# Slot attention and GELU FFN on one core: gelu's first casts move from VectorE to ScalarE, other copies change engine, and the pinned first order is rearranged

## Chip, cores and metric

The kernel runs on one core of a Trainium2 chip. The metric is the device time of one execution in microseconds (us).

## What is computed

There are 8 batches of 8 heads, 576 positions, a head width of 64 and 32 memory slots per head. A softmax over the positions of `phi` gives weights `a`, which sum up `k` and `v` into 32 slots per head. Every position of `q` then attends over these slots. The attention's output, 4608 rows of 512, goes through a feed-forward layer with the exact gelu:

```python
a = exp(phi - max(phi, axis=2)); a = a / (sum(a, axis=2) + 1e-9)
k_m = einsum('bhsm,bhsd->bhmd', a, k); v_m = einsum('bhsm,bhsd->bhmd', a, v)
s = q @ k_m.T / sqrt(64); attn = softmax(s, axis=-1)
x = rows of (attn @ v_m)             # (8*576, 8*64)
h = x @ w_in                         # (4608, 2048)
out = (0.5 * h * (1 + erf(h / sqrt(2)))) @ w_out      # (4608, 512)
```

All inputs are float32 but the two weight matrices, which the kernel receives as float64 numbers viewed as 64-bit integers.

## The kernel before

**Main loop.** For each batch b, `w_in` is first multiplied by the 32 slots of `v` of each head, which gives U (2 x 128 rows, 2048 columns). The product of the attention's probabilities p with U is then h. This is cut along the 2048 columns into 16 steps f of 128 columns. A step (b, f) does the following, with its names in the order:

- `h.b.f.0` and `h.b.f.1` (L679): two halves of 288 positions, each 6 matmuls of 128x288 into one of two PSUM buffers. Six, because a float32 product is made of three products of rounded parts: p_hi U_hi, p_lo U_hi, p_hi U_lo, over two halves of the heads.
- `gelu.b.f.0`, `gelu.b.f.1` (L689, L691, L692): ScalarE writes gelu of the halves to `gf`. The last 64 positions of each batch go to `tails`, and are projected later for two batches together.
- `gh.b.f` (`gelu_hi`, which calls `copy`, L154): a cast of the 128x512 `gf` to the rounded type fp32r.
- `gl.b.f` (L698): VectorE subtracts, gl = gf - gh. There are two buffers each of `gf`, `gh` and `gl`.
- `p.b.f` (`project`, L711): 12 matmuls of 128x512, for each of four blocks of 128 positions gh wo_hi, gh wo_lo and gl wo_hi in this order. They add into the PSUM banks acc0 to acc3.

**Order of the steps.** The steps come as (b=0, f 0 to 7), (b=1, f 0 to 7), (b=0, f 8 to 15), (b=1, f 8 to 15), and then batches 2 to 7 with all 16. After f=7 of batches 0 and 1 the four banks are evicted as partial sums (`o.b.j.7`, tile `part`, L154), and added to the later result when that is evicted.

**What is made once, in the first 140 us.** For each f the loaded weights (`Lwi.f`, `Lwo.f`, into `raw`) are decoded in two 512-wide halves. `dB.f.k` are two ScalarE activations on a half (L201, L202), `dC.f.k` two VectorE steps (L206, L207), `dS.f.k` a shift (L213) on VectorE, `dDi.f` and `dDo.f` an addition on GpSimd each (L223). `dE.f` casts wo_hi (`copy`, ScalarE), and `dF.f` subtracts to get wo_lo (VectorE, L229). There are two buffers `y` for this (tag "wy"). The slots of batches 0 and 1 are made as well: transposes of a (`at`) and their copies (`atc`), `slots`, `km`, `slotsT`, `kT` (for batch 0 into `k_blocks`), and the softmax of the scores (`n_...` for batch 0 in three parts; `score`, `sT`, `max` to `mul`, `pT`, `ph`, `pl` for batch 1). Pieces of U are `Up.b.f.n` (matmuls into the PSUM tile `pu`, n columns of 128; L440), `Uh` (cast, `copy`, ScalarE) and `Ul` (subtraction, VectorE, L642). `pu`, the scores and `slotsT` share one PSUM buffer, "at".

**Who sets the order.** The string START lists the pieces of this part one by one. A piece issues its instructions when it is reached, and for the instructions of this list each engine is chained to go in just this order. Behind the list, a plan with due times and the loop over the steps place the rest, and they are the same in both kernels. A piece may carry an engine's letter behind a colon (d for VectorE, a for ScalarE, p for GpSimd). It replaces the usual engine wherever the piece goes through `eng` or `copy`:

```python
    def eng(usual):
        return {"d": nc.vector, "a": nc.scalar, "p": nc.gpsimd}[st["engine"] or usual]
...
    def gelu_hi(b, f):
        copy("d", g_of("gh", b, f), g_of("gf", b, f))
...
    def do(x):
        x, _, st["engine"] = x.partition(":")
```

A GpSimd `dD` reads what VectorE's `dC` and `dS` wrote. A `dE` waits for that addition, and a `dF` for `dE`; the `y` buffer is free for another f after the `dF`.

Of the kernel before, what the change touches and what calls it, by code (L numbers as in the profile page):

```python
# [19 lines left out]


START = """
Lphi.0.0 Lphi.0.1 Lkv0.1.0 amax.0.0 aexp.0.0 at.0.0.0 Lkv0.0.0 amax.0.1 at.0.0.4 Lq.0.0
Lwi.0 aexp.0.1 at.0.1.4 atc.0.0.4 at.0.1.0 atc.0.1.4 anorm.0 atc.0.0.0 Lwo.0 Lq.0.1
atc.0.1.0 Lwi.1 slots.0.1.0 slots.0.0.0 km.0.0.0 km.0.1.0 slotsT.0.0 kT.0.0 dB.0.0
dC.0.0 n_score.0 Lwo.1 dB.0.1 dC.0.1 n_max.0 n_sub.0 Lkv0.0.1 Lkv0.1.1 dS.0.1 dDo.0
n_exp.0 dB.1.0 n_score.1 n_score.2 dS.0.0 n_sum.0 Lphi.1.1 Lphi.1.0 n_inv.0 n_mul.0
n_T.0 n_max.1 dDi.0 dE.0 slots.0.0.1 slots.0.1.1 n_sub.1 dB.1.1 Lwi.2 dC.1.0 dC.1.1
Lwo.2 dS.1.1 dS.1.0 n_max.2 n_exp.1 n_sum.1 Lkv.1.0.4 n_sub.2 dDo.1 dDi.1 dE.1 Lwo.3
n_exp.2 km.0.0.1 km.0.1.1 slotsT.0.1 kT.0.1 amax.1.1 aexp.1.1 dF.0 Up.0.0.1 Uh.0.0  # L30
amax.1.0 n_inv.1 Ul.0.0 n_mul.1 Lkv.1.1.2 dB.2.0 Up.0.1.1 dC.2.0 Lwi.3 aexp.1.0 Uh.0.1
Lkv.1.0.2 Ul.0.1 n_T.1 dF.1 n_hi.0 dS.2.0 n_sum.2 n_lo.0 Lkv.1.0.0 at.1.0.0 n_inv.2
at.1.1.0 dB.2.1 Lkv.1.0.1 h.0.0.0 dB.3.1 Lkv.1.0.3 dC.2.1 n_hi.1 atc.1.0.0 atc.1.1.0
dDi.2 n_mul.2 n_T.2 at.1.0.4 dS.2.1 Lkv.1.1.3 dB.3.0 n_hi.2 atc.1.0.4 n_lo.1 dDo.2
at.1.1.4 atc.1.1.4 anorm.1 Lwi.4 gelu.0.0.0 n_lo.2 h.0.0.1 dC.3.1 gelu.0.0.1 slots.1.0
gh.0.0 Lkv.1.1.1 dC.3.0 h.0.1.0 km.1.0 dE.2 Up.0.2.1 dS.3.1 Uh.0.2 gl.0.0 Lkv.1.1.0
Lkv.1.1.4 Ul.0.2 dS.3.0 dDo.3 dE.3 dF.2 p.0.0 slots.1.1 dB.4.0 dC.4.0 gelu.0.1.0 Lwo.4
h.0.1.1 Lq.1.0 km.1.1 dDi.3 Lwi.5 dB.4.1 dF.3 slotsT.1 kT.1 h.0.2.0 dC.4.1 dS.4.1 dDo.4
Up.0.3.1 Lwo.5 gelu.0.1.1 gelu.0.2.0 Uh.0.3 dS.4.0 gh.0.1 Ul.0.3 h.0.2.1 gl.0.1 dE.4
Lwi.6 dB.5.0 dDi.4 h.0.3.1 gelu.0.2.1 gh.0.2 score.1.0 Lq.1.1 sT.1.0.1 p.0.1 h.0.3.0  # L40
sT.1.0.0 gelu.0.3.1 Lwo.6 Lwi.7 dC.5.0 dB.5.1 dF.4 Up.0.4.1 dS.5.0 gelu.0.3.0 gl.0.2
max.1.0 gh.0.3 Uh.0.4 p.0.2 sub.1.0 exp.1.0 dDi.5 Ul.0.4 dC.5.1 Up.0.5.1 dS.5.1 dDo.5
h.0.4.1 h.0.4.0 Uh.0.5 dB.6.0 gl.0.3 gelu.0.4.0 Ul.0.5 p.0.3 sum.1.0 dC.6.0 inv.1.0
dS.6.0 gelu.0.4.1 mul.1.0 dDi.6 Lwo.7 score.1.1 h.0.5.1 pT.1.0 gh.0.4 dE.5 sT.1.1.1
ph.1.0 h.0.5.0 Lwi.8 dB.6.1 gelu.0.5.0 sT.1.1.0 gl.0.4 gelu.0.5.1 Up.0.6.1 dC.6.1 gh.0.5
Uh.0.6 dS.6.1 Lwi.9 dF.5 p.0.4 Ul.0.6 dDo.6 dB.7.1 max.1.1 Lwo.9 Up.1.0.4 h.0.6.0 dB.7.0
gl.0.5 Uh.1.0 sub.1.1 dC.7.0 dS.7.0 Ul.1.0 h.0.6.1 pl.1.0 dC.7.1 dE.6 gelu.0.6.0 dDi.7
gelu.0.6.1 dS.7.1 exp.1.1 Lwo.8 p.0.5 gh.0.6 dDo.7 Up.0.7.1 Uh.0.7 gl.0.6 Ul.0.7 sum.1.1
h.1.0.0 inv.1.1 dF.6 h.0.7.0 gelu.0.7.0 dE.7 Up.1.4.4 mul.1.1 dB.8.0 pT.1.1 h.0.7.1
gelu.1.0.0 dC.8.0 ph.1.1 gelu.0.7.1 pl.1.1 p.0.6 h.1.0.1 h.1.1.1 dF.7 gh.0.7 dB.8.1  # L50
gl.0.7 dC.8.1 gelu.1.0.1 dB.9.1 h.1.1.0 gh.1.0 p.0.7 dB.9.0 dS.8.1 gelu.1.1.0 o.0.1.7
dC.9.1 dS.9.1 h.1.2.0 gelu.1.1.1 dS.8.0 Lwi.12 dDo.8 h.1.2.1 Lwi.11 o.0.0.7 dDo.9
o.0.3.7 gl.1.0 Lwo.11 o.0.2.7 dE.9 dC.9.0 p.1.0 dE.8 gelu.1.2.1 gh.1.1 dDi.8 gelu.1.2.0
dF.8 h.1.3.0 dS.9.0 gl.1.1 gh.1.2 dB.11.1 dDi.9 gelu.1.3.0 Lwi.10 h.1.3.1 Lwo.10 dF.9
p.1.1 dC.11.1 Uh.1.4 dS.11.1 gl.1.2 gelu.1.3.1 dB.11.0 gh.1.3 dB.10.0 Ul.1.4 dDo.11
p.1.2 h.1.4.1 h.1.4.0 Lwo.12 gelu.1.4.1 dC.11.0 Lwi.13 gelu.1.4.0 dS.11.0 dC.10.0
# [3 lines left out]
gelu.1.6.1 h.1.7.1 dS.12.0 gh.1.6 dDo.12 gl.1.5 gelu.1.7.1 h.1.7.0 p.1.5 Ul.0.8 gl.1.6  # L60
Lwi.15 dE.12 dB.13.1 h.0.8.0 dDi.12 dF.12 dC.13.1 gelu.1.7.0 h.0.8.1 dB.14.1 dC.14.1
dB.14.0 gh.1.7 gelu.0.8.0 gelu.0.8.1 p.1.6 dS.13.1 Lwo.15 Up.1.8.4 dDo.13 dC.14.0 dE.13
h.0.9.1 dB.13.0 gl.1.7 Uh.1.8 h.0.9.0 dS.14.1 gh.0.8 dC.13.0 dS.13.0 gelu.0.9.1 p.1.7
dDi.13 gelu.0.9.0 dF.13 h.0.10.1 gl.0.8 dB.15.0 o.1.1.7 Ul.1.8 dC.15.0 gelu.0.10.1
# [878 lines left out]
```

## Time and profile before

| | before |
| --- | --- |
| median of 3 runs | 735.46 us (734.17 to 736.1) |
| the profiled execution's own time | 734.68 us |
| its span, first to last instruction | 732.9 us |
| mean granted TensorE clock | 0.985 |
| TensorE busy | 707.0 us, 4958 matmuls |
| VectorE busy | 395.2 us, 706 instructions |
| ScalarE busy | 335.5 us, 693 instructions |
| GpSimd busy | 52.3 us, 45 instructions |

PE is TensorE, PEld its weight loads (which run beside the matmuls), DVE is VectorE, ACT ScalarE, POOL GpSimd. Durations are of one profiled execution. A row of the timeline holds the start (us from the span's start), the duration (us), the engine, the line, the operation, the output <- the inputs, and in brackets how long the engine had waited and for whom. A row of the groups ends in busy time (us) and mean duration (ns) of one, then the idle time of the engine ahead of them and what ended it. A row of the waits says who waited <- for whom: us in total, times, longest. A row of the stretches holds the window, its length, and for PE, PEld, DVE, ACT and POOL the busy time and, in brackets, the number of instructions; then the granted clock, the DMA share and GB/s.

### The profile page before, as it was taken

The numbers are of one execution on the slowest core, as the hardware profiler recorded it, in microseconds if no ns is written. First come the engines' busy times: TensorE is split into PE (matmuls) and PEld (weight loads), VectorE is DVE, ScalarE is ACT, GpSimd is POOL, SyncE is SP. The second block draws the span as 40 slices with busy tenths as digits, with TensorE's granted clock in tenths as the row PEclk, the third lists the DMA queues.
The fourth block names the chain that finished last, engine by engine and source line by source line (L and its number), as shares of the span: only waits on it lengthen the run. The fifth ranks groups of instructions, "written<-read, shape, count | busy, mean of one in ns | idle before, by whom it ended". The sixth has DMA issues, their size and how long they took to land.

```text
span 732.9 us, 12219 instructions
## 1 busy us (share of the span) xinstructions
PE 707.0 (96%) x4958; PEld 576.7 (79%) x4958; DVE 395.2 (54%) x706; ACT 335.5 (46%) x693; POOL 52.3 (7%) x45
## 2 busy tenths in 40 slices
...
PEclk7699999999999999999999999999999999999999
...
GB/s 303 321 212 192 87 203 154 1 1 200 125 105 87 143 104 94 33 205 62 33 1 64 190 62 33 1 205 27 36 2 58 47 33 1 0 58 1 1 1 72
DMA packets 42584, 65.15 MB, mean 89 GB/s; under 512 B 2848, under 2 KB 24992, under 8 KB 42528
## 3 DMA queue, kind: packets, MB, share of 16 engines
...
## 4 chain that ended last, share of the span: by engine, by line
PE 80%; DVE 9%; DMA 3%; ACT 3%; issue 2%; SPq 1%; POOL 1%; ACTq 0%; POOLq 0%; DVEq 0%
PE acc L711 42%; PE h L679 24%; PE tacc L711 6%; PE pu L440 4%; DMA q<-qT 2%; DVE raw L207 2%; PE psc L382 1%; DVE y L206 1%; DVE gh L154 1%; DVE y L213 1%; PE psc L440 1%; DVE wo_lo L229 1%; DVE gl L698 1%; PE pk L382 1%; PE psc L457 1%
## 5 line engine op out<-in xcount | busy, mean ns | idle before, releaser
L679 PE MATMUL h<-p_hi,U 128*128 128x288 f32 x1024 | 206.2, 299 | 5.4 <-ACT tails L692 2.8
L711 PE MATMUL acc<-wo_hi,gh 128*128 128x512 f32 x512 | 203.5, 398 | 1.1 <-DVE part L154 1.1
L711 PE MATMUL acc<-wo_hi,gl 128*128 128x512 f32 x512 | 201.6, 395 | 2.4 <-DVE gl L698 2.4
L711 PE MATMUL acc<-wo_lo,gh 128*128 128x512 f32 x512 | 201.2, 393 | 0.0
L679 PEld LDWEIGHTS h<-p_hi,U 128*128 128x128 f32 x1024 | 164.1, 188 | 25.6 <-issue 4.8
L154 DVE CAST gh<-gf 128x512 fp32r<-128x512 f32 x128 | 57.8, 451 | 204.9 <-ACT gf L691 202.8
L689 ACT ACTIVATE gf<-h 128x288 f32<-128x288 f32 x128 | 52.6, 411 | 231.0 <-issue 168.4
L711 PEld LDWEIGHTS acc<-wo_hi,gh 128*128 128x128 f32 x512 | 96.1, 188 | 36.4 <-DVE gh L154 7.5
L711 PEld LDWEIGHTS acc<-wo_hi,gl 128*128 128x128 f32 x512 | 95.9, 188 | 27.2 <-DVE gl L698 5.2
L711 PEld LDWEIGHTS acc<-wo_lo,gh 128*128 128x128 f32 x512 | 96.1, 188 | 17.4 <-issue 0.4
L679 PE MATMUL h<-p_lo,U 128*128 128x288 f32 x512 | 109.5, 295 | 0.0
L698 DVE TENSOR_TENSOR gl<-gf,gh 128x512 fp32r<-128x512 f32 x128 | 91.8, 717 | 8.0
L679 PEld LDWEIGHTS h<-p_lo,U 128*128 128x128 f32 x512 | 83.1, 188 | 0.7 <-issue 0.7
L691 ACT ACTIVATE gf<-h 128x224 f32<-128x224 f32 x128 | 45.6, 356 | 46.9 <-PE h L679 41.2
L642 DVE TENSOR_TENSOR U<-pu,U 128x1024 fp32r<-128x1024 f32 (+2 forms) x39 | 40.0, 1025 | 14.9 <-ACT U L154 14.9
L689 ACT ACT_TABLE_LOAD x30 | 38.5, 1283 | 14.2 <-PE h L679 6.7
L154 ACT CAST U<-pu 128x1024 fp32r<-128x1024 f32 (+2 forms) x39 | 33.6, 863 | 17.9 <-PE pu L440 17.2
L440 PE MATMUL pu<-w_in_sb,kT 64*32 64x512 f32 (+2 forms) x624 | 36.7, 528 | 2.8 <-DVE U L642 1.4
L223 POOL TENSOR_TENSOR y<-y,raw 128x512 int32<-128x512 int32 x16 | 24.8, 1550 | 70.9 <-DVE y L213 52.2
L692 ACT ACTIVATE tails<-h 128x64 f32<-128x64 f32 x128 | 28.5, 223 | 0.0
L548 DVE STREAM_TRANSPOSE sT<-psc 128x288 f32<-128x288 f32 x28 | 11.8, 461 | 30.2 <-PE psc L382 24.5
L201 ACT ACTIVATE y<-raw 128x512 f32<-128x512 f32 (+1 forms) x33 | 22.9, 694 | 10.6 <-DVE wo_lo L229 4.3
...
## 6 DMA issues: line engine op xcount, KB each, us to landing
...
```

The source lines that it names most:

```text
L154: return e.copy(dst, src) if e is nc.scalar else e.tensor_copy(dst, src)
L201: nc.scalar.activation(y, high.bitcast(F32), AF.Abs, scale=2.0**16)
L207: nc.vector.scalar_tensor_tensor(low, high, -(2**31), low, op0=ALU.bitwise_and, op1=ALU.bitwise_or)
L223: nc.gpsimd.tensor_tensor(w, y, low, op=ALU.add)
L440: nc.tensor.matmul(ps[g][M * j : M * j + M], st["kT", b][rows, t, M * j : M * j + M], moving[rows, j, :], start=True, stop=True,)
L642: nc.vector.tensor_sub(u[:, :, 1], st["pu", b, f], u[:, :, 0].bitcast(F32))
L679: i = nc.tensor.matmul(h[:, :HS], u[g][w], x[:, g, :], start=(n == 0), stop=(n == 3 * G - 1))
L689: nc.scalar.activation(gf[:, :HS], h[:, :HS], AF.Gelu)
L691: nc.scalar.activation(gf[:, HS:], h[:, : MAIN - HS], AF.Gelu)
L692: nc.scalar.activation(tails()[:, f, b % 2], h[:, MAIN - HS : HS], AF.Gelu)
L698: nc.vector.tensor_tensor(g_of("gl", b, f), g_of("gf", b, f), g_of("gh", b, f).bitcast(F32), op=ALU.subtract)
L711: nc.tensor.matmul(acc, x, w[:, f, :], start=(first and n == 0), stop=(last and n == 2))
```

## The change

Only START changes, and one line is added to it, so that a line L154 of before is L155 of after. Three things change in it:

- 18 `gh` casts get ":a" and go to ScalarE: f=0 to 9 of batch 0 and f=0 to 7 of batch 1. `gh.0.10` and `gh.0.11` stay on VectorE, and so do all the `gh` behind the list.
- Other copies change their engine. From ScalarE to VectorE go five copies of aT (`atc.0.0.0`, `atc.0.0.4`, `atc.0.1.4`, `atc.1.0.4`, `atc.1.1.4`), the two of `kT.0.0`, the U casts `Uh.0.3`, `Uh.0.6`, `Uh.1.4`, `Uh.1.8` and `Uh.0.12`, the wo_hi cast `dE.12`, and the evictions `o.1.1.7` and `o.1.3.7`. From VectorE to ScalarE go the evictions `o.0.0.7`, `o.1.0.7` and `o.1.2.7`.
- The list is rearranged: the loads of phi and kv, the softmax of batch 0, the decode (f=9 now ahead of f=8, and 13, 14, 12, 15 in place of 12, 13, 14, 15), and the halves of `h` and the pieces of U among the projects.

The part of the diff around steps 1.3 to 1.6:

```diff
-dS.10.0 dB.10.1 Lwo.13 h.1.5.0 gl.1.3 h.1.5.1 dC.10.1 dS.10.1 dDi.11 dDi.10 dDo.10 p.1.3
-dE.11 gh.1.4 gelu.1.5.0 dF.11 dB.12.1 h.1.6.0 dE.10 gelu.1.5.1 Lwo.14 Up.0.8.4 dB.12.0
-gl.1.4 dC.12.1 Uh.0.8 Lwi.14 dS.12.1 gh.1.5 dF.10 p.1.4 gelu.1.6.0 dC.12.0 h.1.6.1
...
+gelu.1.5.0 h.1.5.1 dF.11 p.1.3 gelu.1.5.1 h.1.6.0 dB.13.1 dS.10.0 gh.1.4:a dS.10.1
+gl.1.4 dDi.10 h.1.6.1 Lwi.13 Up.0.8.4 dDo.10 dC.13.1 gelu.1.6.0 Lwi.14 dB.13.0 p.1.4
+gh.1.5:a dE.10 dC.13.0 dS.13.0 Uh.0.8 dS.13.1 h.1.7.1 dF.10 Ul.0.8 gl.1.5 dDo.13
```

In the orders below, a tile `gf_1_4_1217` is `gf` of b=1, f=4; the last number only numbers the tiles. In tiles of `h` and `gf`, the order is batch, (half,) f. Here is ScalarE's order behind gelu of step 1.4 before:

```order
L689 ACTIVATE gf_1_4_1217<-h_1_0_4_1209 128x288
L201 ACTIVATE y_10_1185<-raw_10_1150 128x512
L202 ACTIVATE raw_10_1150<-raw_10_1150 128x512
L154 CAST wo_hi_77<-y_11_1144 128x512
L689 ACTIVATE gf_1_5_1269<-h_1_0_5_1232 128x288
L201 ACTIVATE y_12_1272<-raw_12_1082 128x512
L202 ACTIVATE raw_12_1082<-raw_12_1082 128x512
L154 CAST wo_hi_77<-y_10_1185 128x512
L691 ACTIVATE gf_1_5_1269<-h_1_1_5_1241 128x224
```

And ScalarE's order at the same place after:

```order
L692 ACTIVATE gf_1_4_1212<-h_1_1_4_1203 128x224
L693 ACTIVATE tails_469<-h_1_1_4_1203 128x64
L155 CAST wo_hi_77<-y_11_1133 128x512
L690 ACTIVATE gf_1_5_1243<-h_1_0_5_1236 128x288
L692 ACTIVATE gf_1_5_1243<-h_1_1_5_1245 128x224
L693 ACTIVATE tails_469<-h_1_1_5_1245 128x64
L202 ACTIVATE y_13_1274<-raw_13_1210 128x512
L203 ACTIVATE raw_13_1210<-raw_13_1210 128x512
L155 CAST gh_1_4_1278<-gf_1_4_1212 128x512
L690 ACTIVATE gf_1_6_1305<-h_1_0_6_1267 128x288
L202 ACTIVATE y_13_1274<-raw_13_1210 128x512
```

The cast of gh.1.4 now stands on ScalarE behind the first two decode steps of f=13 (`y_13`, `raw_13`), where before f=12 was decoded.

VectorE's order from gl.1.4 to gl.1.5 before:

```order
L698 TENSOR_TENSOR gl_1_4_1299<-gf_1_4_1217,gh_1_4_1267 128x512
L206 TENSOR_SCALAR y_12_1272<-y_12_1272 128x512
L207 SCALAR_TENSOR_TENSOR raw_12_1082<-raw_12_1082 128x512
L213 TENSOR_SCALAR y_12_1272<-y_12_1272 128x512
L154 CAST gh_1_5_1306<-gf_1_5_1269 128x512
L229 TENSOR_TENSOR wo_lo_78<-y_10_1185,wo_hi_77 128x512
L206 TENSOR_SCALAR y_12_1272<-y_12_1272 128x512
L207 SCALAR_TENSOR_TENSOR raw_12_1082<-raw_12_1082 128x512
L213 TENSOR_SCALAR y_12_1272<-y_12_1272 128x512
L154 CAST gh_1_6_1342<-gf_1_6_1321 128x512
L698 TENSOR_TENSOR gl_1_5_1345<-gf_1_5_1269,gh_1_5_1306 128x512
```

VectorE's order between the same two after:

```order
L699 TENSOR_TENSOR gl_1_4_1281<-gf_1_4_1212,gh_1_4_1278 128x512
L207 TENSOR_SCALAR y_13_1274<-y_13_1274 128x512
L208 SCALAR_TENSOR_TENSOR raw_13_1210<-raw_13_1210 128x512
L207 TENSOR_SCALAR y_13_1274<-y_13_1274 128x512
L208 SCALAR_TENSOR_TENSOR raw_13_1210<-raw_13_1210 128x512
L214 TENSOR_SCALAR y_13_1274<-y_13_1274 128x512 x2
L230 TENSOR_TENSOR wo_lo_78<-y_10_1181,wo_hi_77 128x512
L643 TENSOR_TENSOR U_0_2_1301<-pu_0_8_1292,U_0_2_1301 128x2x512
L699 TENSOR_TENSOR gl_1_5_1340<-gf_1_5_1243,gh_1_5_1323 128x512
```

The casts gh.1.5 and gh.1.6 have left the stretch, and the subtraction Ul.0.8 of U (`U_0_2`) now stands ahead of gl.1.5.

The last place is the eviction of bank acc0 of batch 1 (`part_1_0`), behind which project 0.8 can begin. VectorE's order there before:

```order
L206 TENSOR_SCALAR y_15_1490<-y_15_1490 128x512
L207 SCALAR_TENSOR_TENSOR raw_15_1372<-raw_15_1372 128x512
L213 TENSOR_SCALAR y_15_1490<-y_15_1490 128x512
L213 TENSOR_SCALAR y_14_1397<-y_14_1397 128x512
L154 COPY part_1_2_1530<-acc_1_0_2_1109 128x512
L154 CAST gh_0_9_1532<-gf_0_9_1463 128x512
L154 COPY part_1_0_1534<-acc_1_0_0_1107 128x512
```

ScalarE's order at that place after:

```order
L202 ACTIVATE y_15_1484<-raw_15_1395 128x512
L203 ACTIVATE raw_15_1395<-raw_15_1395 128x512
L690 ACTIVATE gf_0_9_1505<-h_0_0_9_1489 128x288
L155 COPY part_1_2_1507<-acc_1_0_2_1138 128x512
L692 ACTIVATE gf_0_9_1505<-h_0_1_9_1496 128x224
L693 ACTIVATE tails_469<-h_0_1_9_1496 128x64
L155 CAST gh_0_9_1526<-gf_0_9_1505 128x512
L155 COPY part_1_0_1535<-acc_1_0_0_1136 128x512
```

The copy of acc0, and with it the cast gh.0.9 and the copy of acc2, have gone from VectorE to ScalarE, where they stand among the decode of f=15 and gelu of step 0.9.

More of the change, by code (lines that the diff above doesn't have):

```diff
@@ L22 @@
 START = """
[L23 to L56, printed above, removed]
-dS.10.0 dB.10.1 Lwo.13 h.1.5.0 gl.1.3 h.1.5.1 dC.10.1 dS.10.1 dDi.11 dDi.10 dDo.10 p.1.3
-dE.11 gh.1.4 gelu.1.5.0 dF.11 dB.12.1 h.1.6.0 dE.10 gelu.1.5.1 Lwo.14 Up.0.8.4 dB.12.0
@@ L59 @@
-gl.1.4 dC.12.1 Uh.0.8 Lwi.14 dS.12.1 gh.1.5 dF.10 p.1.4 gelu.1.6.0 dC.12.0 h.1.6.1
[L60 to L64, printed above, removed]
@@ L65 @@
-o.1.3.7 h.0.10.0 dDo.14 h.0.11.0 dS.15.0 dS.14.0 Up.0.12.2 o.1.2.7 gh.0.9 o.1.0.7 p.0.8
-dDi.15 gelu.0.10.0 h.0.11.1 dE.14 dB.15.1 gl.0.9 gelu.0.11.0 gh.0.10 dC.15.1 gl.0.10
-Uh.0.12 gelu.0.11.1 dF.14 dS.15.1 dDi.14 p.0.9 Ul.0.12 gh.0.11 gl.0.11 p.0.10
+Lphi.0.1 Lphi.0.0 Lkv0.1.0 amax.0.1 Lkv0.0.0 aexp.0.1 amax.0.0 aexp.0.0 at.0.0.4
+at.0.1.0 anorm.0 Lq.0.0 at.0.1.4 Lwi.0 Lwo.0 atc.0.1.0 atc.0.0.4:d at.0.0.0 atc.0.0.0:d
+atc.0.1.4:d slots.0.1.0 Lq.0.1 slots.0.0.0 km.0.1.0 km.0.0.0 dB.0.0 slotsT.0.0 kT.0.0:d
@@ new lines @@
+dC.0.0 dS.0.0 n_score.0 n_max.0 n_sub.0 dB.0.1 n_exp.0 Lwi.1 Lwo.1 dC.0.1 dS.0.1
+Lkv0.0.1 n_sum.0 n_inv.0 n_score.1 dB.1.0 dB.1.1 n_mul.0 Lkv0.1.1 n_score.2 dC.1.0 n_T.0
+n_max.1 dC.1.1 Lphi.1.1 n_sub.1 slots.0.0.1 Lphi.1.0 Lwi.2 dDi.0 n_max.2 dS.1.1 dS.1.0
+Lwo.2 Lkv.1.0.2 slots.0.1.1 n_exp.1 n_sum.1 n_sub.2 dDo.0 dE.0 n_inv.1 n_exp.2 km.0.0.1
+km.0.1.1 slotsT.0.1 amax.1.1 dDo.1 n_mul.1 dE.1 dDi.1 kT.0.1 Lwi.3 dF.0 Up.0.0.1
+aexp.1.1 amax.1.0 Uh.0.0 n_T.1 dB.2.0 aexp.1.0 Ul.0.0 Up.0.1.1 n_sum.2 Lkv.1.1.1
@@ new lines @@
+Lkv.1.0.3 n_inv.2 n_mul.2 dF.1 Lkv.1.0.4 n_T.2 Uh.0.1 n_hi.0 Ul.0.1 at.1.0.0 Lkv.1.0.0
+dB.2.1 at.1.1.0 n_hi.2 dC.2.0 Lwo.3 dS.2.0 n_lo.0 h.0.0.0 n_lo.2 dDi.2 Lkv.1.0.1 dC.2.1
+dB.3.0 atc.1.0.0 atc.1.1.0 n_hi.1 gelu.0.0.0 dS.2.1 at.1.1.4 Lwi.4 anorm.1 n_lo.1
+Lkv.1.1.0 Lwo.4 at.1.0.4 atc.1.1.4:d atc.1.0.4:d h.0.0.1 dC.3.0 dB.3.1 dC.3.1 gelu.0.0.1
+slots.1.0 gh.0.0:a Lkv.1.1.2 dDo.2 km.1.0 dE.2 h.0.1.0 Up.0.2.1 gl.0.0 Lkv.1.1.3
+Lkv.1.1.4 gelu.0.1.0 dF.2 Lwi.5 dB.4.0 dS.3.1 Uh.0.2 dS.3.0 p.0.0 Ul.0.2 slots.1.1
@@ new lines @@
+dB.4.1 dC.4.0 dDo.3 dDi.3 km.1.1 dE.3 h.0.1.1 dC.4.1 Lq.1.0 dS.4.1 gelu.0.1.1 slotsT.1
+h.0.2.0 Lwo.6 kT.1 Up.0.3.1 gh.0.1:a h.0.2.1 dF.3 gelu.0.2.0 Uh.0.3:d Ul.0.3 dDo.4 Lwo.5
+gelu.0.2.1 dS.4.0 h.0.3.0 score.1.0 gl.0.1 dDi.4 Lwi.6 dB.5.0 gelu.0.3.0 sT.1.0.1
+gh.0.2:a sT.1.0.0 dE.4 dC.5.0 dS.5.0 p.0.1 gl.0.2 dB.5.1 Up.0.4.1 dDi.5 h.0.3.1 max.1.0
+Uh.0.4 Ul.0.4 dF.4 h.0.4.1 sub.1.0 dC.5.1 gelu.0.3.1 Lq.1.1 gh.0.3:a dS.5.1 Up.0.5.1
+gelu.0.4.1 Lwo.7 p.0.2 gl.0.3 Lwi.9 Uh.0.5 Ul.0.5 exp.1.0 sum.1.0 inv.1.0 h.0.4.0 dDo.5
@@ new lines @@
+score.1.1 dB.6.0 mul.1.0 p.0.3 h.0.5.0 dC.6.0 Lwi.7 dS.6.0 dB.6.1 gelu.0.4.0 gh.0.4:a
+dE.5 pT.1.0 sT.1.1.1 h.0.5.1 Lwo.9 sT.1.1.0 Lwo.8 dDi.6 ph.1.0 Up.0.6.1 gl.0.4
+gelu.0.5.0 dC.6.1 dF.5 dS.6.1 gelu.0.5.1 Uh.0.6:d gh.0.5:a max.1.1 dB.7.1 dB.7.0 p.0.4
+Ul.0.6 dDo.6 dE.6 Lwi.8 gl.0.5 sub.1.1 dC.7.0 dC.7.1 Up.1.0.4 h.0.6.0 dS.7.0 exp.1.1
+pl.1.0 Uh.1.0 gelu.0.6.0 h.0.6.1 dDi.7 Ul.1.0 gelu.0.6.1 p.0.5 Up.0.7.1 Uh.0.7 dS.7.1
+dDo.7 h.1.0.0 dF.6 gh.0.6:a Ul.0.7 h.0.7.0 dB.9.1 sum.1.1 Up.1.4.4 gelu.1.0.0 h.0.7.1
```

16 lines of the change are left out of this document (added).

## The prediction

> **What bounds the kernel now.** I read the page first, then the stretches of the pinned order, then who waits for whom in them. The page's first part and the slices of the granted clock:
>
> ```profile
> span 732.9 us, 12219 instructions
> PE 707.0 (96%) x4958; PEld 576.7 (79%) x4958; DVE 395.2 (54%) x706; ACT 335.5 (46%) x693; POOL 52.3 (7%) x45
> PEclk7699999999999999999999999999999999999999
> ```
>
> TensorE is busy for 96% of the span, so over the whole run only its waits can be won, and VectorE's 54% says nothing yet. The busy time by stretch (us; busy time and instructions of each engine, granted clock, DMA share, GB/s) shows where the waits are:
>
> ```profile
> 0.00:15.00 15.00, 10.29 (x122) 8.90 (x122) 3.98 (x12) 7.65 (x16) 0.96 (x7) 0.86 0.89 287
> 15.00:41.00 26.00, 19.15 (x225) 15.37 (x227) 24.44 (x56) 17.26 (x39) 7.90 (x6) 0.69 0.91 294
> 41.00:118.00 77.00, 72.09 (x551) 55.49 (x552) 73.42 (x126) 50.24 (x108) 32.54 (x20) 1.00 0.48 158
> 118.00:139.00 21.00, 19.77 (x128) 15.70 (x129) 18.20 (x31) 14.40 (x34) 8.05 (x6) 1.00 0.41 135
> 203.00:733.00 530.00, 524.15 (x3500) 433.32 (x3498) 239.74 (x420) 211.33 (x440) 1.22 (x4) 1.00 0.19 61
> ```
>
> From 41 to 118 us VectorE (third) is busy 73.42 of 77 us, while ScalarE (fourth) has 26.8 us free. After 203 us VectorE has more than half of its time free. The pinned order ends at about 139 us, where project f=9 of batch 0 starts on TensorE; from that instruction on, TensorE's order is the same in both kernels. So the change is worth what it does to the start of that instruction. TensorE's waits from 40 to 140 us (us in total, times, longest):
>
> ```profile
> PE acc L711 <- DVE gl L698: 2.4, 4, 0.9
> PE h L679 <- ACT gf L689: 1.3, 2, 0.8
> PE acc L711 <- DVE part L154: 1.1, 1, 1.1
> PE h L679 <- DVE U L642: 1.1, 1, 1.1
> PE pu L440 <- DVE km L396: 0.8, 1, 0.8
> ```
>
> These 6.7 us are all that can be won there, and 5.4 of them are waits for VectorE. The last one for `gl` is at project 1.5 (batch 1, f=5), at the end of the crowded stretch:
>
> ```profile
> 116.59 0.40 PE L711 MATMUL acc<-wo_lo,gh 128*128 128x512 f32 x1
> 117.88 0.50 PE L711 MATMUL acc<-wo_hi,gl 128*128 128x512 f32 x1 [0.89 <-DVE gl L698]
> ```
>
> The two matmuls that use `gh` have gone by; the third waits for `gl`. VectorE's queue, not gelu, is what is late: in 41 to 118 us VectorE itself waited little (first rows), while ScalarE stood waiting for the decode's other engines (last three):
>
> ```profile
> DVE gh L154 <- ACT gf L691: 1.5, 1, 1.5
> DVE y L206 <- ACT y L201: 1.3, 3, 0.8
> ACT y L201 <- DVE wo_lo L229: 4.3, 2, 4.0
> ACT wo_hi L154 <- POOL y L223: 3.8, 3, 1.4
> ACT gf L691 <- DVE gl L698: 3.0, 1, 3.0
> ```
>
> **VectorE's queue up to gl.1.5.** A busy engine's cost is the step from one start to the next, so prices come from runs of the timeline without idle time:
>
> ```profile
> 66.87 0.42 DVE L154 CAST gh<-gf 128x512 fp32r<-128x512 f32 x1
> 67.20 0.42 DVE L213 TENSOR_SCALAR y<-y 128x512 int32<-128x512 int32 x1
> 67.54 0.68 DVE L229 TENSOR_TENSOR wo_lo<-y,wo_hi 128x512 fp32r<-128x512 f32 x1
> 68.14 0.41 DVE L642 TENSOR_TENSOR U<-pu,U 128x256 fp32r<-128x256 f32 x1
> 68.48 0.74 DVE L559 TENSOR_REDUCE mx<-sT 128x18 f32<-128x576 f32 x1
> ...
> 71.81 1.21 DVE L642 TENSOR_TENSOR U<-pu,U 128x1024 fp32r<-128x1024 f32 x1
> 72.95 0.95 DVE L610 TENSOR_TENSOR p_lo<-pT,p_hi 128x576 fp32r<-128x576 f32 x1
> ```
>
> A `gh` cast takes 67.20 - 66.87 = 0.33 us, a shift 0.34, a 512-wide two-input step 0.60 (67.54 to 68.14), a U step 0.34 (256 elements) or 1.14 (1024). Between gl.0.0 and gl.1.5 VectorE's list loses 14 `gh` casts (14 x 0.33 = 4.6) and one eviction (0.60). It gains the U casts 0.3 and 0.6 (0.34 each) and 1.4 (1.14), priced by the subtraction of the same shape that also reads PSUM; the subtraction Ul.0.8 (1.14), which now stands ahead of gl.1.5; and one shift (0.34). The decode of f=12 is exchanged for that of f=13 at no cost. Sum: -5.2 + 3.3 = **-1.9 us**.
>
> The 20 GpSimd additions in this stretch hold VectorE up. From the timelines of the two engines, and the group of the 14 casts of 41 to 118 us:
>
> ```profile
> 94.18 0.68 DVE L698 TENSOR_TENSOR gl<-gf,gh 128x512 fp32r<-128x512 f32 x1
> 94.78 1.54 DVE L154 CAST gh<-gf 128x512 fp32r<-128x512 f32 x1
> 96.24 0.68 DVE L229 TENSOR_TENSOR wo_lo<-y,wo_hi 128x512 fp32r<-128x512 f32 x1
> 94.34 1.70 POOL L223 TENSOR_TENSOR w_in_sb<-y,raw 128x512 int32<-128x512 int32 x1 [1.91 <-DVE y L213]
> 59.47 1.55 POOL L223 TENSOR_TENSOR y<-y,raw 128x512 int32<-128x512 int32 x1 [2.79 <-DVE y L213]
> 59.77 0.41 DVE L642 TENSOR_TENSOR U<-pu,U 128x256 fp32r<-128x256 f32 x1
> L154 DVE CAST gh<-gf 128x512 fp32r<-128x512 f32 x14 | 8.8, 632 | 1.5 <-ACT gf L691 1.5
> ```
>
> A `gh` that meets an addition is held until it ends: 1.54 us in place of 0.42. The mean of the 14 is 0.632, so 14 x (0.632 - 0.42) = 3.0 us were such holding. With `gh` gone an addition meets the neighbour, so most of this stays. But the last pair held nothing: the U subtraction beside the addition, with one input in PSUM, took its usual 0.41. The three PSUM-fed casts that VectorE receives here are 0.34 + 0.34 + 1.14 = 1.8 us of its time; of 20 additions in 77 us, 1.8 x 20 / 77 = 0.5 start beside one, each saving 1.54 - 0.42 = 1.1: **-0.5 us**, between 0 and -3.0.
>
> The Trainium skill (GPSIMD Engine Reference, Key points) says that GpSimd shares its SBUF interfaces with VectorE and contends with instructions in a 2-port mode or with two SBUF inputs. Both pairs agree. By that rule no U step is ever held, the moved Ul.0.8 neither: 2.9 us of such steps in place of 1.8, and -0.8 in place of -0.5, an estimate that the sum doesn't use.
>
> **Waits between the two engines.** The 1.5 us in which VectorE stood at gh.0.2 for gelu was bare idle time; now VectorE does its other work while ScalarE catches up: **-1.5 us**. In exchange, `gl` now waits for ScalarE's queue. The dearest place in the new queues is gh.1.4. There the decode of f=13 stands ahead of it and first needs the buffer that dF.11 on VectorE frees (the 4.0 us that ScalarE waited at the like place before, harming nobody). After dF.11 VectorE has two shifts (0.7 us) ahead of gl.1.4; ScalarE needs two decode steps and the cast. Their prices, and those of the copies that change hands:
>
> ```profile
> L201 ACT ACTIVATE y<-raw 128x512 f32<-128x512 f32 x32 | 21.8, 680 | 10.3 <-DVE wo_lo L229 4.3 <-issue 2.7 <-POOL w_in_sb L223 1.9
> L154 ACT CAST wo_hi<-y 128x512 fp32r<-128x512 f32 x16 | 9.8, 620 | 9.0 <-POOL y L223 9.0
> L154 ACT CAST U<-pu 128x1024 fp32r<-128x1024 f32 x29 | 29.5, 1019 | 15.4 <-PE pu L440 14.9 <-POOL w_in_sb L223 0.5
> ```
>
> About 0.6 + 0.6 + 0.6 less 0.7 is 1.1 us of idle VectorE. Then gelu.1.6.0 needs gl.1.4's buffer, and the second half of the decode comes behind it: another 0.5. Together **+1.6 us**. ScalarE's load itself is covered: 14 casts at 0.62 (the nearest SBUF cast, wo_hi) are +8.7 us, U casts leaving it -1.8, so 57 of 77 us busy. Without that cover, every us would land on `gl`. Bounds of this term: 0 with no new wait at all, +7.4 for rival two.
>
> **The end of the pinned order.** So gl.1.5 comes 1.9 + 0.5 + 1.5 - 1.6 = 2.3 us earlier. TensorE has one half `h` more to do after it than before (0.8 us). The 1.1 us that project 0.8 waited for the eviction of acc0 should go: the copy moves to ScalarE, and TensorE has five pieces instead of four between projects 1.7 and 0.8. Sum: -2.3 + 0.8 - 1.1 = **-2.6 us**. If the decode of f=15 ahead of that copy delays it, the 1.1 us stay.
>
> **The first 41 us.** Three copies of aT and two of k_blocks go to VectorE, which has 11 us free of the first 15, and so cost nothing while the load of q bounds the start:
>
> ```profile
> 6.32 10.59 DMA q<-qT
> ```
>
> The second half of the scores starts when it has landed, at 17 us, in both. Behind that, the reordered softmax of batch 0 gives n_sub.1 later and n_mul.1 earlier, which I take as 0, between -1 and +1.5 (the clock, 0.69 in 15 to 41 us, may return to full later if TensorE's gaps grow).
>
> The profiled execution took 734.68 us, its span 732.9. Less 2.6 that is 732.1; the median of the runs shown, 735.46, is 0.8 above it, so **732.9 us**. A measurement of this kernel can tell about 0.3%, 2.2 us, from no change; the forecast lies just beyond that.
>
> **The rivals.** *One: it nets out.* The wait that goes at gh.0.2 comes back at another `gl` (+1.5), since each `gl` now has a second engine's queue ahead of it, and the holding is unchanged (+0.5): 732.9 + 2.0 = 734.9. For it: VectorE gives up 1.9 us of 77, little. Against it: ScalarE's 27 free us.
>
> *Two, slower: ScalarE's waits are passed on to VectorE.* From 41 to 118 us ScalarE waited 4.3 + 3.8 + 3.0 = 11.1 us for decode and `gl` in the rows above, and that cost nothing while VectorE made `gh` itself. Now 14 casts stand in that queue. If x us of these waits reach `gl`, gl.1.5 moves by x - 3.9 and the end by x - 4.2: at x = 1.6 it is the forecast, from 4.2 no gain, from 6.4 a loss that shows. With two thirds, 7.4 us, it is +3.2, or 738.7 us. Against it: the casts are placed right behind their gelu in most places, and waits of 1 us have slack in projects where `gl` is early. By a rule of the Trainium skill (ScalarE: Activation LUTs, in the steps of the ACTIVATE: ScalarE is closer to PSUM, VectorE to SBUF) the change goes against the grain, since SBUF casts go to ScalarE and PSUM casts to VectorE. The trace agrees in the prices, 0.62 against 0.42 for the one and 1.14 against 1.02 for the other.
>
> *That the change does nothing* is excluded: the order shows the casts on the other engine.
>
> **How the numbers follow.** Forecast 0.48, rival one 0.32, rival two 0.20. The first is faster by over 0.3%, the second within it, the third slower: 0.48, 0.32, 0.20. The range goes down to 732.9 - 2.5 (the rest of the holding) - 0.9 (most of the start's gain), 729.5, and up to 737.5, most of the way to rival two, so that about one in ten is left out on each side.
>
> **What would show it.** Right: the waits of TensorE for `gl` from 40 to 140 us fall from 2.4 to under 1, those for part to 0, and project 0.9 starts near 136 us in place of 138.5; ScalarE's busy time there grows by some 8 us. Wrong: VectorE idle for `gh` from ScalarE by more than 4 us in total, or the first project later than 41.3 us by over 1.5.

## The result, and the profile after

The changed kernel takes 724.13 us (median of 4 runs, 724.06 to 726.52) against 735.67 us before on the same chip: a ratio of 0.9855 (95% interval 0.983 to 0.9879), 11.5 us less. The forecast was 732.9 us with a range from 729.5 to 737.5, so the direction was right; the size was more than four times too small, and the time lies outside the range. The profiled execution took 724.06 us, its span is 722.3. The page's first part and the slices of the granted clock after:

```profile
span 722.3 us, 12207 instructions
PE 706.1 (98%) x4958; PEld 577.9 (80%) x4958; DVE 385.3 (53%) x700; ACT 340.3 (47%) x699; POOL 51.3 (7%) x45
PEclk8699999999999999999999999999999999999999
```

TensorE's busy time is nearly the same (706.1 and 707.0); the gain is nearly all waiting that is gone. VectorE lost 9.9 us of busy time and ScalarE gained 4.8. Where the waiting went is seen when the time between two instructions of the crowded part is compared: the first matmuls of project 0.0 and of project 0.9, in the timeline before (first) and after (second):

```profile
41.34 0.49 PE L711 MATMUL acc<-wo_hi,gh 128*128 128x512 f32 x1
...
138.54 0.40 PE L711 MATMUL acc<-wo_hi,gh 128*128 128x512 f32 x1
```

```profile
39.51 0.50 PE L712 MATMUL acc<-wo_hi,gh 128*128 128x512 f32 x1
...
128.56 0.39 PE L712 MATMUL acc<-wo_hi,gh 128*128 128x512 f32 x1
```

From one to the other took 97.20 us before and takes 89.05 after: 8.15 us. Project 0.0 comes 1.83 us earlier, and behind project 0.9, where the order is the same, 0.6 is won: 10.6 us of span. In the table of the stretches, before (first) and after (second), TensorE's busy time is the first column behind the length:

```profile
41.00:139.00 98.00, 91.86 (x678) 71.19 (x679) 91.61 (x156) 64.64 (x141) 40.58 (x26) 1.00 0.46 153
```

```profile
39.00:129.00 90.00, 89.94 (x680) 71.71 (x679) 82.23 (x146) 72.08 (x155) 39.68 (x26) 1.00 0.49 165
```

Before, TensorE was idle for 6.1 of these 98 us; after, for 0.06 of 90. The rest of what was won in the stretch, some 2 us, lies in TensorE's busy time, 91.86 and 89.94 us for nearly the same number of matmuls. For TensorE's waits from 40 to 138 us, of which five were shown before, the view after has no row at all. So this part runs at TensorE's own speed now, and no waiting is left to win in it.

### The profile page after: what moved, and what is told of

Read it like the earlier page. It is cut to its first block, busy times and chain, and to the rows that moved or that the text cites. A ratio compares the mean times of both kernels' runs of the same rounds, so it can differ in the third digit from the quotient of the medians.

```text
span 722.3 us, 12207 instructions
## 1 busy us (share of the span) xinstructions
PE 706.1 (98%) x4958; PEld 577.9 (80%) x4958; DVE 385.3 (53%) x700; ACT 340.3 (47%) x699; POOL 51.3 (7%) x45
## 4 chain that ended last, share of the span: by engine, by line
PE 90%; DVE 5%; issue 2%; ACT 1%; DMA 1%; POOL 0%; ACTq 0%; POOLq 0%; DVEq 0%
PE acc L712 47%; PE h L680 27%; PE tacc L712 6%; PE pu L441 4%; PE psc L383 1%; PE psc L441 1%; PE pk L383 1%; DVE raw L208 1%; DMA kv<-kv 1%; DVE y L207 0%; DVE gl L699 0%; DVE y L214 0%; DMA phi<-phiT 0%; PE psc L458 0%; DVE wo_lo L230 0%
## 5 line engine op out<-in xcount | busy, mean ns | idle before, releaser
L155 DVE CAST gh<-gf 128x512 fp32r<-128x512 f32 x110 | 46.7, 425 | 199.4 <-ACT gf L692 198.4
L699 DVE TENSOR_TENSOR gl<-gf,gh 128x512 fp32r<-128x512 f32 x128 | 91.7, 717 | 10.6 <-ACT gh L155 2.0
L155 ACT CAST U<-pu 128x1024 fp32r<-128x1024 f32 (+2 forms) x34 | 30.4, 893 | 16.2 <-PE pu L441 16.2
L224 POOL TENSOR_TENSOR w_in_sb<-y,raw 128x512 int32<-128x512 int32 x16 | 25.3, 1583 | 35.8 <-DVE y L214 35.8
```

Of the source, the lines that this page charges most:

```text
L155: return e.copy(dst, src) if e is nc.scalar else e.tensor_copy(dst, src)
L224: nc.gpsimd.tensor_tensor(w, y, low, op=ALU.add)
L699: nc.vector.tensor_tensor(g_of("gl", b, f), g_of("gf", b, f), g_of("gh", b, f).bitcast(F32), op=ALU.subtract)
```

## The experiments

Each was timed against the kernel before, on the same chip. The changed kernel lost its casts, its order or its other letters one at a time, and the kernel before got them one at a time. Then VectorE got the lost time back in two forms, and the last runs ask what the other letters and the start are worth. In the table further down, "0.0" and "0.9" are the starts of the two projects in the profiled execution and "between" is what lies between them.

**One: the changed kernel with the casts back on VectorE.**

```diff
-gh.0.0:a
+gh.0.0
...
-gh.1.7:a
+gh.1.7
```

> The changed kernel with its 18 gh casts put back on VectorE; order and all other engine letters stay. Theory one, the casts leaving VectorE are what counts (between gl.0.0 and gl.1.5 VectorE's own work fell by 2.0 us, and the holding by GpSimd's additions by 6.8): most of the gain goes again, 730 to 734 us, and TensorE waits for gl from 40 to 130 us again. Theory two, the new order does it whatever engine casts: 723 to 726 us.

730.97 us (ratio 0.9947, 0.9932 to 0.9961): 6.8 us of the gain is gone, 4.2 stays. Theory one holds for most of it. TensorE waits again, in the same window:

```profile
PE h L680 <- DVE U L643: 1.9, 2, 1.4
PE acc L712 <- DVE gl L699: 1.4, 2, 1.0
PE pu L441 <- DVE sT L549: 0.8, 1, 0.8
```

**Two: the kernel before with the 18 casts on ScalarE**, and nothing else.

```diff
-gh.0.0
+gh.0.0:a
...
-gh.1.7
+gh.1.7:a
```

> The kernel before with nothing but the same 18 gh casts on ScalarE, order unchanged. Theory one: most of the gain, 727 to 731 us, since the holding goes with the casts. Theory two: no gain or a loss, 735 to 740 us, because the casts stand in ScalarE's old queue behind decode steps that wait.

725.78 us (0.9878, 0.9855 to 0.9901): 9.4 us from the casts alone, in the old order, in which nothing was placed for them. The two projects and TensorE's only wait from 40 to 138 us:

```profile
41.17 0.50 PE L711 MATMUL acc<-wo_hi,gh 128*128 128x512 f32 x1
...
130.26 0.40 PE L711 MATMUL acc<-wo_hi,gh 128*128 128x512 f32 x1
```

```profile
PE h L679 <- DVE U L642: 0.3, 1, 0.3
```

Between them lie 89.09 us: the casts alone bring the stretch to the same floor as the whole change, and the start (41.17) is the old one.

**Three and four: the new order with the casts' letters only, and with no letter.**

```diff
-atc.0.0.4:d
+atc.0.0.4
...
-kT.0.0:d
+kT.0.0
```

> The changed kernel with all other engine letters taken off (copies of aT, kT, U casts, dE.12 and evictions on their usual engine); gh casts stay on ScalarE. Theory one: 724 to 727 us, the other letters are worth little. Rival: the other letters keep ScalarE's queue short enough, and without them it costs 3 us or more, 727 to 731.

> The changed kernel's order with no engine letter at all. Theory one: 731 to 736 us, as the first experiment or worse. Theory two: 724 to 728 us.

727.07 us (0.9894, 0.9879 to 0.9909) and 733.33 us (0.9978, 0.9969 to 0.9987). The new order alone is worth 1.8 us, with the casts on ScalarE 8.1, with the other letters on top 11.5. By its number the rival of the third run holds: the other letters are worth some 3 us in this order. Its reason, a shorter queue on ScalarE in general, does not: the projects start at 42.54 and 131.86 us in the third, so 89.32 lie between them, as after. The letters win in the start, not in the stretch.

**Five: VectorE gets its casts back, as spare work.** In the second experiment's kernel each of the 18 casts on ScalarE is followed by one on VectorE that nobody needs:

```diff
     def gelu_hi(b, f):
         copy("d", g_of("gh", b, f), g_of("gf", b, f))
+        if st["engine"] == "a":
+            nc.vector.tensor_copy(g_of("gl", b, f), g_of("gf", b, f))
```

> The second experiment's kernel (order of before, 18 gh casts on ScalarE, 725.8 us) with a spare cast on VectorE at each of the 18 places: the same 128x512 gf, written to gl's buffer, which gl then overwrites. VectorE's list is that of before again, ScalarE keeps gh. Theory one, what the move gained is VectorE's time (bare casts and what GpSimd's additions hold them): 733 to 736 us, the whole gain gone. Rival: the gain is that gh is made earlier and apart from VectorE's queue: 726 to 729 us.

733.92 us (0.9989, 0.9977 to 1.0001): within 0.3% of before. Where `gh` is made does not matter; that VectorE spends the time does.

**Six and nine: the same with a step that GpSimd does not hold.** The sixth writes a maximum over 128x288 to a small new tile, the ninth one over 128x256 to a tile that exists. The ninth's lines against the fifth's:

```diff
-            nc.vector.tensor_copy(g_of("gl", b, f), g_of("gf", b, f))
+            nc.vector.tensor_reduce(
+                warm_exp, g_of("gf", b, f)[:, 2 * P :].rearrange("p (a m) -> p a m", m=M),
+                axis=AX.X, op=ALU.max,
+            )
```

> As the fifth, but the spare step is a maximum over 128x288 of the same gf into a small tile, about 0.33 us like the bare cast, and of a kind that ran beside additions at its usual time in the traces (0.74 us for 128x576 in both cases). So VectorE gets the bare time back without the holding. If the holding of the casts (3.2 us between gl.0.0 and gl.1.5) is part of the gain: 2.5 to 4 us under the fifth, 730 to 732 us. If only the casts' bare time counts: the same as the fifth within 1 us.

> The sixth again, with the spare maximum over 128x256 written to a tile that is there already, since the small new tile of the sixth moved all later tiles by 36 bytes and every projection took 2.80 us in place of 2.77 to the end of the run. The sixth's stretch from project 0.0 to project 0.9 was 93.5 us (fifth 96.4, second 89.1). If the holding of the casts is 3 us of the gain: a stretch near 93.3 us, projections of 2.77 us, and 729.5 to 731 us, some 3 to 4 under the fifth. If only bare time counts: 733 to 735 us. If the slower projections do not go with the tile: 733 us or more, with 2.80 us each.

The sixth took 734.82 us (0.9997, 0.9985 to 1.0009), which by its expectation would mean that holding counts for nothing. But its stretch was 93.46 us, nearly 3 below the fifth's, and the time was lost again behind it: the projects' matmuls ran slower to the end. From 200 to 700 us in the sixth, and then in the ninth:

```profile
L718 PE MATMUL acc<-wo_hi,gh 128*128 128x512 f32 x377 | 151.0, 401 | 0.0
L718 PE MATMUL acc<-wo_lo,gh 128*128 128x512 f32 x377 | 148.8, 395 | 0.0
```

```profile
L716 PE MATMUL acc<-wo_hi,gh 128*128 128x512 f32 x380 | 150.9, 397 | 0.0
L716 PE MATMUL acc<-wo_lo,gh 128*128 128x512 f32 x380 | 149.2, 393 | 0.0
```

The ninth, without the new tile, took 729.66 us (0.9928, 0.9908 to 0.9949), with 93.00 us between the projects. Its spare steps take 0.41 us each beside additions and away from them (14 with a mean of 0.406), the fifth's casts 0.633:

```profile
L697 DVE TENSOR_REDUCE warm_exp<-gf 128x8 f32<-128x256 f32 x14 | 5.7, 406 | 1.5 <-ACT gf L691 1.5
```

```profile
L697 DVE CAST gl<-gf 128x512 fp32r<-128x512 f32 x14 | 8.9, 633 | 1.5 <-ACT gf L691 1.5
```

So 733.92 - 729.66 = 4.3 us are the casts' holding, and 729.66 - 725.78 = 3.9 us their bare time. Over the 18 casts together, holding is about half of what they cost.

**Seven: the kernel before without the additions.**

```diff
-        eng("d").tensor_single_scalar(y, y, 3, op=ALU.logical_shift_left)
+        for x in k or (0, 1):
+            y = w = parts(f, (x,))[2].bitcast(I32)
+            if x == 0:
+                w = w_in_sb[:, :, f * P : (f + 1) * P].bitcast(I32)
...
+            eng("d").tensor_single_scalar(w, y, 3, op=ALU.logical_shift_left)
...
-        nc.gpsimd.tensor_tensor(w, y, low, op=ALU.add)
```

> The kernel before without GpSimd's additions of the decode (the shift writes the weight itself, so the lowest bits of the weights are left out). All holding goes, 13.7 us between gl.0.0 and gl.1.5, and an addition's time goes out of each decode. If the holding is what makes VectorE late: project 0.0 to project 0.9 falls from 97.2 us to TensorE's own 89, and the time to 724 to 728 us. If VectorE's own work is what counts: not under 731 us.

What the addition puts in is the sign of each weight as well as its lowest bits (`dC` joins both in `raw`), so this kernel leaves out the signs too and computes something else; the other steps stay. 725.34 us (0.9873, 0.9853 to 0.9894), with 89.39 us between the projects: taking the holder away brings TensorE to its floor too, with all casts on VectorE. An addition's time in each decode goes with it, so this shows that VectorE has enough time without the holding, not that the holding was the only cause.

**Eight, thirteen and fourteen: the letter of kT.0.0.** The eighth takes only this letter off the changed kernel, the thirteenth leaves only this one and the casts', the fourteenth adds it to the second experiment.

```diff
-kT.0.0:d
+kT.0.0
```

> The changed kernel with only the two copies of kT.0.0 back on ScalarE. If they are why the start was won (TensorE waited 2.8 us for k_blocks without any of the letters, 1.0 with them): the first scores come 1.8 us later, project 0.0 near 42 us in place of 39.5, and the time is 726 to 727.5 us. If the copies of aT or q's load set the start: 723.5 to 725 us.

> The changed kernel with the letters of the 18 gh casts and of kT.0.0 alone (without any 727.1, with all but kT.0.0 726.9, with all 724.1). If kT.0.0 is all that the other letters are worth: 724 to 725 us, project 0.0 near 39.7 us. If it needs the copies of aT with it: 725.5 to 727 us.

> The order of before with the letters of the 18 gh casts and of kT.0.0 (with the casts alone 725.8, with all letters 729.3). If kT.0.0 is what costs in the old order: 728 to 730 us. If it is the copies of aT, the U casts and the evictions: 725 to 726 us, and below 725 if kT.0.0 wins its 0.7 us wait for k_blocks here too.

They took 726.89 (0.989, 0.9871 to 0.9909), 724.45 (0.9858, 0.9845 to 0.9871) and 726.7 us (0.9892, 0.9878 to 0.9906). The thirteenth and the third differ in this letter alone, by 2.6 us with intervals that don't meet: it is what the other letters are worth. In the old order it wins nothing: the fourteenth lies between its two expected ranges, 0.9 us over the second with intervals that overlap. The timeline of ScalarE in the third says why:

```profile
12.65 0.66 ACT L202 ACTIVATE y<-raw 128x512 f32<-128x512 f32 x1 [3.29 <-DMA raw<-w_in]
13.21 0.66 ACT L203 ACTIVATE raw<-raw 128x512 int32<-128x512 uint32 x1
13.77 0.52 ACT L155 COPY k_blocks<-tn 64x128 f32<-64x128 f32 x2
```

And ScalarE before, in the same place:

```profile
11.30 0.53 ACT L154 COPY k_blocks<-tn 64x128 f32<-64x128 f32 x2 [3.40 <-PE tn L406]
12.37 0.66 ACT L201 ACTIVATE y<-raw 128x512 f32<-128x512 f32 x1 [0.54 <-DMA raw<-w_in]
```

The new order puts the first decode (`dB.0.0`) ahead of the copy, and that waits for a weight to land. On ScalarE the copy then stands behind that wait, and the first scores with it (14.38 us in the third, 12.58 in the changed kernel):

```profile
14.38 7.91 PE L458 MATMUL psc<-k_blocks,q 128*128 128x64 f32 x36 [2.77 <-ACT k_blocks L155]
```

```profile
12.58 2.79 PE L458 MATMUL psc<-k_blocks,q 128*128 128x64 f32 x16 [0.95 <-DVE k_blocks L155]
```

**Ten: the order of before with all letters.**

```diff
-kT.0.0
+kT.0.0:d
...
-o.1.3.7
+o.1.3.7:d
```

> The order of before with all engine letters of the change. If the start is set by q's second half and by the softmax behind it in this order, whatever engine copies: project 0.0 at 41 us as before, and 724.5 to 726.5 us, like the second. If the letters win the start in this order too (2.9 us in the new one): 722.5 to 723.5 us, under the changed kernel.

729.32 us (0.993, 0.9908 to 0.9952, six runs from 727.88 to 733.15): neither, but 3.5 us worse than the second. By the medians kT.0.0 costs 0.9 of it (fourteen), so most is due to the copies of aT, the U casts, dE.12 or the evictions; which of them was not tried. Its profile is of the slowest of the six runs, so it is a weak witness: project 0.0 starts at 43.49 us and the stretch is 91.43, each 2.3 over the second's.

**Eleven: every other cast.**

```diff
-gh.0.0
+gh.0.0:a
 gh.0.1
-gh.0.2
+gh.0.2:a
```

> The order of before with every other one of the 18 casts on ScalarE (nine: f even). Each cast took 0.33 us bare and 0.2 held. If the gain goes by VectorE's time until TensorE's own time is reached: 9 x 0.53 = 4.8 of 9.4 us, 729 to 732 us. If a few crowded places make it: near 735 or near 726.

730.41 us (0.9926, 0.9904 to 0.9948) and 92.62 us between the projects. By the medians half of the casts give 4.8 of the 9.4 us, which fits a gain that goes with the number of casts and not with one place. The profile is a weaker witness: it is of the slowest of the four runs (732.25 us), and of the 4.6 us that its stretch is shorter, 2.8 are a later project 0.0 (44.17 us). In the account of the next section its own time is 2.3 us less than before and its held time only 0.1 less, so this run does not show that every cast takes its share of the holding away.

**Twelve: f=15 decoded once.**

```diff
-... gelu.0.11.1 dS.15.1 gl.0.10 p.0.9 Ul.0.12 gh.0.11:d p.0.10 gl.0.11
+... gelu.0.11.1 dS.15.1 dDo.15 gl.0.10 p.0.9 Ul.0.12 dE.15 gh.0.11:d p.0.10 gl.0.11 dF.15
```

> The changed kernel without what lies behind the pinned list in both: there the plan decodes f=15 a second time, whole (two ScalarE steps of 1024, three of VectorE and the additions), because the list leaves its last three pieces out. They are put into the list and the second decode goes. TensorE waited 1.8 us for ScalarE's tails at 152 us in the changed kernel. If that ScalarE time is what it waited for: 1 to 2 us less, 722 to 723 us. If the wait is set by the exponentials there: 724 us, no change.

725.59 us (0.9866, 0.9847 to 0.9884): no change. TensorE's wait of 1.6 us for `tails` at the first half of step 1.8, behind project 0.14, is still there with two ScalarE steps fewer ahead of it, so those were not what it waited for. What sets it stays open.

**Fifteen: the start of before.** The list of before up to project 0.0, and behind it what is left of the changed list, with its letters.

```diff
-Lphi.0.1 Lphi.0.0 Lkv0.1.0 amax.0.1 Lkv0.0.0 aexp.0.1 amax.0.0 aexp.0.0 at.0.0.4
+Lphi.0.0 Lphi.0.1 Lkv0.1.0 amax.0.0 aexp.0.0 at.0.0.0 Lkv0.0.0 amax.0.1 at.0.0.4
```

> The list of before up to project 0.0 (gh.0.0 on ScalarE), then the changed kernel's list and letters. If the new start is worth the 1.8 us that the profiles show (project 0.0 at 41.3 and 39.5 us): 725.5 to 726.5 us. If that difference was the throttle's clock between 36 and 42 us, which differs from execution to execution: 724 to 724.7 us.

728.12 us (0.9906, 0.989 to 0.9923, six runs from 725.97 to 729.53), outside both ranges. The new start is worth 4 us against this, more than the 1.8 that the two profiles of before and after show. In this run's profile project 0.0 starts at 42.94 us, 3.4 later than after, and 89.59 us lie between the projects. The old start scatters: in the eight profiles that have it without the letters of aT and kT, project 0.0 starts between 41.0 and 44.2 us, in the four with the new start and kT.0.0 on VectorE between 39.2 and 40.0. No version was clearly faster than the changed kernel; the thirteenth, with 16 letters fewer, is as fast.

## Why the prediction was wrong, step by step

The sum was made at `gl.1.5` on VectorE. The same account on six kernels: the stretch from gl.0.0 to gl.1.5 on VectorE, in us. "Own" is each instruction at the step that it takes undisturbed (from the runs without idle time before), "held" is what steps took beyond that, "idle" the gaps between instructions. A rest of 2.1 us counts as held even in the seventh, without additions, so differences are what is to be read.

| kernel | stretch | own | held | idle | 0.0 | 0.9 | between |
| --- | --- | --- | --- | --- | --- | --- | --- |
| before | 75.0 | 57.7 | 13.7 | 3.6 | 41.34 | 138.54 | 97.20 |
| casts alone (two) | 68.7 | 53.0 | 10.6 | 5.0 | 41.17 | 130.26 | 89.09 |
| spare casts (five) | 74.5 | 57.6 | 13.2 | 3.7 | 41.29 | 137.70 | 96.41 |
| spare maxima (nine) | 71.5 | 57.6 | 10.2 | 3.7 | 41.01 | 134.01 | 93.00 |
| new order and other letters, casts on VectorE (one) | 75.1 | 60.1 | 10.2 | 4.8 | 40.04 | 135.83 | 95.79 |
| after | 69.0 | 55.8 | 6.7 | 6.5 | 39.51 | 128.56 | 89.05 |

**What bounds: right, but the cap was too low.** VectorE's queue was what TensorE waited for, as the fifth run shows. "These 6.7 us are all that can be won there" was wrong: 8.15 us were won between the projects. The idle time that went is 6.0 us of it; the other 2 us were in TensorE's busy time, which the waits view doesn't list.

**VectorE's own queue, -1.9: right.** 57.7 to 55.8 us.

**The holding, -0.5: this is the step that failed.** The forecast said that "an addition meets the neighbour, so most of this stays", and counted only three new casts as neighbours that aren't held. Held time fell by 7.0 us in place of 0.5, beyond the bound of 3.0. The bound took in only the casts' own holding, 3.2 us in this account; the other 3.8 us came off steps that VectorE kept. With the casts alone it fell by 3.1, all that the casts' own holding was, and the other steps were held no more than before (13.7 less the casts' 3.2 is 10.5; 10.6 in the second). The neighbours that took the additions were steps that VectorE had all along. The same place on VectorE in both, first before and then in the second experiment:

```profile
93.84 0.42 DVE L213 TENSOR_SCALAR y<-y 128x512 int32<-128x512 int32 x1
94.18 0.68 DVE L698 TENSOR_TENSOR gl<-gf,gh 128x512 fp32r<-128x512 f32 x1
94.78 1.54 DVE L154 CAST gh<-gf 128x512 fp32r<-128x512 f32 x1
```

```profile
93.85 0.42 DVE L213 TENSOR_SCALAR y<-y 128x512 int32<-128x512 int32 x1
94.19 0.68 DVE L698 TENSOR_TENSOR gl<-gf,gh 128x512 fp32r<-128x512 f32 x1
94.79 1.21 DVE L642 TENSOR_TENSOR U<-pu,U 128x1024 fp32r<-128x1024 f32 x1
```

And GpSimd's addition there in the second experiment (before it starts at 94.34):

```profile
94.50 1.55 POOL L223 TENSOR_TENSOR y<-y,raw 128x512 int32<-128x512 int32 x1 [2.06 <-ACT y L201]
```

The addition starts under `gl` and holds the step after. Before, that was a cast, and 1.1 us were lost; now the wide subtraction of U has moved up into the place and takes its usual 1.21 us. Of the wide U subtractions from gl.0.0 to gl.1.5 none of two starts under an addition before, both in the second experiment, and all three after; at 1.1 us each that is 2.2 of the 3.1 and 3.3 of the 7.0 us. The new order with its other letters does the same without the casts' move (13.7 to 10.2 in the first experiment, all three there), and the casts' leaving takes the rest.

The forecast counted half an addition that starts beside one of the new U casts. Counted in the timelines of VectorE and GpSimd, with narrow and wide steps of U together, 4 of 8 start under an addition before, 6 of 8 in the second, 9 of 12 in the first and 11 of 12 after, two of the three new casts among them. Seven more at 1.1 us are 7.7 us, near the 7.0. In the eleventh, with nine casts gone, the count is 3 of 8 and the held time stays. The count and the held time go the same way, but not in fixed proportion (five more in the first experiment, for 3.5 us). That the steps of U explain these differences is read from the traces and not separated by a run; that holding is some 4 us of the casts' price is shown by the fifth and the ninth.

By the Trainium skill (GPSIMD Engine Reference, Key points), additions contend with VectorE's 2-port modes and with steps of two SBUF inputs; the spare maximum, one SBUF input at 0.41 us beside additions, agrees. The cast that was held for 1.54 us has one SBUF input as well, so it falls under the rule only if it ran in such a mode, which no run here shows. What the forecast did not do is to go through the new neighbours of every addition, where the order was known.

**The waits between the engines, +0.1: too small by 2.8, and harmless.** VectorE's idle time rose from 3.6 to 6.5 us. The new wait of `gl` for `gh` came as forecast, 1.5 us against 1.6. Others came with it. VectorE's waits from 39 to 108 us after:

```profile
DVE U L643 <- ACT U L155: 2.1, 3, 0.9
DVE gl L699 <- ACT gh L155: 1.5, 2, 1.2
DVE y L207 <- ACT y L202: 1.5, 2, 1.3
```

None reached TensorE.

**The end of the pinned order, -0.3.** From the start of gl.1.5 (116.04, then 107.95) to project 0.9 it was 22.50 us and is 20.61, -1.9. The one more half of `h` (+0.8) and the eviction's wait (-1.1) came as forecast. What it left out is that gl.1.5 itself was held; before, and then after:

```profile
116.04 1.78 DVE L698 TENSOR_TENSOR gl<-gf,gh 128x512 fp32r<-128x512 f32 x1
```

```profile
107.95 0.68 DVE L699 TENSOR_TENSOR gl<-gf,gh 128x512 fp32r<-128x512 f32 x1
```

That is another -1.1; the last -0.5 was not traced.

**The start, 0: wrong.** That the load of q bounds the start is not borne out by the second experiment: there the second half of the scores began 1.76 us earlier than before, and project 0.0 only 0.17 earlier (41.17 and 41.34). The rows, before and then in the second:

```profile
17.04 5.36 PE L457 MATMUL psc<-k_blocks,q 128*128 128x64 f32 x24 [1.47 <-DMA q<-qT]
```

```profile
15.28 5.14 PE L457 MATMUL psc<-k_blocks,q 128*128 128x64 f32 x23 [0.24 <-DMA q<-qT]
```

The second's granted clock was lower behind that (0.75 against 1.00 from 36 to 42 us, in the last section), which may have taken some of the 1.76 us, so what bounds the start stays open. The new order wins 1.8 us in the profiles and 4 in the medians, and only with kT.0.0 on VectorE (with it on ScalarE project 0.0 starts at 41.4 to 42.7 us).

**The sum.** Project 0.9 came 10.0 us earlier in place of 2.6. Of the 7.4 us that the forecast missed, the holding is 6.5, the start 2.1 (gl.0.0 at 41.06 and 38.92 us) and the end of the pinned order 1.6; the waits between the engines took 2.8 back.

**The rivals.** Rival two, ScalarE's waits passed on, did not come about even in the old order, where the casts stand in the queue as it was: VectorE's idle time rose by 1.4 us there. By the Trainium skill (ScalarE: Activation LUTs, Step-by-step: what each stage is for) the casts went to the farther engine, and they do cost more there, 0.625 us against 0.42; it still won 9.4 us, because ScalarE had the time and VectorE had not. Rival one, that it nets out, is refuted by the same run. Of the signs given, the waits for `gl` fell from 2.4 to nothing and those for `part` to nothing, and ScalarE's busy time grew by 7.4 us (64.64 to 72.08 in the stretches above), as said; project 0.9 came at 128.6 us where 136 was forecast.
